# Top-k attention and a gated MLP on one core: a rounding step rewritten, and four steps of a slot reordered

## The chip, the cores and the metric

The kernel runs on one core of a Trainium2 chip. The metric is the device time of one execution in microseconds (us), from the first to the last instruction of the core. The profile is one profiled execution of the same program.

## The reference

Two layers in a row. The first is attention over 8 batches, 8 heads, 576 positions and head size 64, in which each row keeps its 32 largest scores:

```python
scores = scale * np.matmul(q, k.transpose(0, 1, 3, 2))
kth = np.partition(scores, -top_k, axis=-1)[..., -top_k:-top_k + 1]
mask = scores >= kth
scores = np.where(mask, scores, -1000000000.0)
scores = scores - np.max(scores, axis=-1, keepdims=True)
attn = np.exp(scores)
attn = attn / (np.sum(attn, axis=-1, keepdims=True) + 1e-09)
return np.matmul(attn, v).astype(np.float32)
```

The result is laid out as 4608 tokens of 512 values and goes through the second layer, whose weights are 512 x 2048 and 2048 x 512 and come in float64:

```python
h = x @ w_in
g = h * (1.0 / (1.0 + np.exp(-1.702 * h)))
return (g @ w_out).astype(np.float32)
```

## The kernel before

Engines are named PE (TensorE), DVE (VectorE), ACT (ScalarE), POOL (GpSimd) and SP (SyncE, which issues all loads and stores here). Each works through its own queue in program order, and the order of the program is written out by hand: nothing is moved by a scheduler.

**Slots.** The work is cut into 144 slots, 18 for each batch. A slot is 128 query rows of a pair of heads; the last 64 rows of two pairs share an "ends" slot. Even batches run their 16 full slots first and the two ends slots last, odd batches the other way round. The function `slot(n)` issues for each engine what belongs to slot n, in a software pipeline. DVE selects the 32 largest of the rows of slot n (`topk`, 14 operations: MAX8 on L241, MATCH_REPLACE8 on L244, two heads in turn). For slot n-1, POOL makes the two bounds (L260, L261), ACT the exponentials (L269, L271), DVE the division's reciprocal (L280, L282, after topk's operation 5). In the first ten slots POOL then scales an identity (`by`, L286) that the turning on PE multiplies with (L302); from slot SETTLED (9) on ACT and POOL scale the exponentials themselves (L288, L289) and PE turns them (L300). ACT copies the turned blocks out (L310), PE multiplies with the values (L332), ACT copies the result (L344). For slot n+2, PE makes the scores (L225) and ACT copies them out (L232).

**The second layer in the same slots.** When 128 tokens are complete, four slots get a quarter each of the hidden layer (`hidden`, 32 matmuls, L373), at the slot's end. In the next slot ACT takes the tanh (L390) and the gate multiplies it with the hidden values: up to slot 9 and after the last attention slot on DVE straight from PSUM (L406), in between on POOL (L403, L404) after ACT has copied the hidden values (L393). `project` (8 matmuls, L421) comes two slots later at the earliest.

**q and k.** `load` fetches a pair's q or k, `prepare` turns it: four PE transposes into one of the two PSUM buffers of `ps_t` (L193) and one ACT copy (L195). The prepare of k also turns the last 64 positions of q and k together (L199, a second buffer of ps_t) and copies them out (L200, L202). The buffers of ps_t also take the turned blocks and the results of the values, in rotation. A table, READY, says in which slot each is prepared. In even batches every q and k has a slot of its own; in odd batches the third pair's q and k share one slot, and the fourth pair's another:

```python
    READY = (((-9, -8), (-7, -6), (-5, -4), (-3, -2)), ((-7, -6), (-5, -4), (-3, -3), (-2, -2)))
```

From slot 7 on (`settled`), the prepares are issued after topk and ahead of the projection and the turning, and the scores after the values; in slots 0 to 6 the prepares and the scores are issued ahead of topk.

**The weights.** In slots 0 to 8 the float64 weights are rounded to float32, 32 pieces of 128 x 512, three or four a slot (two in slot 0). Their raw words stand in `raws`, 8 buffers; the loads of a slot's pieces are issued one slot ahead. A piece goes through ACT (magnitude of the high word, "size", L142), DVE (shift left by 3, L143, between topk's operations from the eighth on), ACT (L145 "low" and L144 "sign") and, in the next slot, POOL (two operations of 128 x 512, L138 and L139, "finish").

Of the kernel before, what the change touches and what calls it, by code (L numbers as in the profile page):

```python
# [9 lines left out]
ALU = mybir.AluOpType  # L10
ENG = mybir.EngineType
F32 = mybir.dt.float32
U32 = mybir.dt.uint32
# [3 lines left out]
P = 128  # L17
# [11 lines left out]
def kernel(  # L29
# [24 lines left out]
    nc = tc.nc  # L54
# [13 lines left out]
    PIECE = 512  # L68
# [12 lines left out]
    const = ctx.enter_context(tc.tile_pool(name="const", bufs=1))  # L81
# [20 lines left out]

    ident = const.tile([P, P], F32, name="ident")
    make_identity(nc, ident[:])
    win = const.tile([P, CC, DFF], F32, name="win")
    wout = const.tile([P, FC, C], F32, name="wout")

# [14 lines left out]
    def round_piece(n):  # L122

        c, g = pieces[n]
        dst = wout[:, g, :] if c is None else win[:, c, g * PIECE : (g + 1) * PIECE]
        words = raw.pop(n)[:].rearrange("p (n w) -> p n w", w=2)
        low, high = words[:, :, 0], words[:, :, 1].bitcast(F32)
        bits, whole = dst.bitcast(U32), dst.bitcast(I32)

        def finish():
            nc.gpsimd.tensor_tensor(out=whole, in0=whole, in1=low.bitcast(I32), op=ALU.add)  # L138
            nc.gpsimd.tensor_tensor(out=dst, in0=dst, in1=high, op=ALU.mult)  # L139

        return {
            "size": lambda: nc.scalar.activation(dst, high, AF.Abs, scale=REBASE),  # L142
            "shift": lambda: nc.vector.tensor_scalar(bits, bits, 3, None, op0=ALU.logical_shift_left),  # L143
            "sign": lambda: nc.scalar.activation(high, high, AF.Sign),  # L144
            "low": lambda: nc.scalar.mul(out=low.bitcast(I32), in_=low, mul=2.0**-29),  # L145
            "finish": finish,
        }
# [37 lines left out]
    def prepare(name, b, hp):  # L185
        src = loaded.pop((name, b, hp))


        before = 0 if name == "q" else TAIL
        dst = qkt.tile([P, S + before], F32, name=f"{name}_t")  # L190
        full = ps_t.tile([P, 512], F32, name="tp")
        for t in range(NF):
            nc.tensor.transpose(full[:, t * P : (t + 1) * P], src[:, t, :, :], ident[:])  # L193
        scale = SCALE if name == "q" else 1.0
        nc.scalar.mul(out=dst[:, before : before + FULL], in_=full[:], mul=scale)  # L195
        (qT if name == "q" else kT)[b, hp] = dst
        if name == "k":
            ends = ps_t.tile([P, 512], F32, name="tp")
            nc.tensor.transpose(ends[:, 0:P], loaded.pop(("ends", b, hp))[:], ident[:])  # L199
            nc.scalar.mul(out=qT[b, hp][:, FULL:S], in_=ends[:, 0:TAIL], mul=SCALE)  # L200
            for to in (0, before + FULL):
                nc.scalar.copy(out=dst[:, to : to + TAIL], in_=ends[:, TAIL:P])  # L202
# [12 lines left out]
    def scores(n):  # L215
        b, t, hps = slots[n]
        ps = [ps_s.tile([P, 2, 512], F32, name="s_ps") for _ in range(2)]
        if t < NF:
            parts = [(i, 0, slice(0, P), slice(t * P, (t + 1) * P)) for i in range(2)]
        else:  # L220
            parts = [(i, p, slice(p * TAIL, (p + 1) * TAIL), slice(FULL, S)) for i, p in ((0, 0), (1, 1), (0, 1), (1, 0))]
        for c in range(2):
            for i, p, rows, cols in parts:
                on = slice(i * D, (i + 1) * D)
                nc.tensor.matmul(  # L225
                    ps[i][rows, c, 0:HALF],
                    lhsT=qT[b, hps[p]][on, cols],
                    rhs=kT[b, hps[p]][on, FIRST[i] + c * HALF : FIRST[i] + (c + 1) * HALF],
                )
        sc = st[n]["sc"] = scp.tile([P, 2, S], F32, name="sc")  # L230
        for i in range(2):
            nc.scalar.copy(out=sc[:, i, :].rearrange("p (c k) -> p c k", c=2), in_=ps[i][:, :, 0:HALF])  # L232
# [22 lines left out]
    def bounds(n):  # L255

        top = st[n]["top"]
        cut = st[n]["cut"] = small.tile([P, 2], F32, name="cut")
        low = st[n]["low"] = small.tile([P, 2], F32, name="low")
        nc.gpsimd.tensor_scalar(cut[:], top[:, :, TOPK - 1], -1.0, None, op0=ALU.mult)  # L260
        nc.gpsimd.tensor_tensor(out=low[:], in0=top[:, :, TOPK - 1], in1=top[:, :, 0], op=ALU.subtract)  # L261

    def exponentials(n):

        sc, cut, low = st[n]["sc"], st[n]["cut"], st[n]["low"]
        pr = st[n]["pr"] = prp.tile([P, 2 * S], F32, name="pr")
        den = st[n]["den"] = small.tile([P, 2], F32, name="den")
        for i in range(2):
            nc.scalar.activation(sc[:, i, :], sc[:, i, :], AF.Prelu, bias=cut[:, i : i + 1], alpha=HUGE)  # L269
        for i in range(2):  # L270
            nc.scalar.activation(  # L271
                pr[:, i * S : (i + 1) * S], sc[:, i, :], AF.Exp, bias=low[:, i : i + 1],
                accum_out=den[:, i : i + 1],
            )
# [37 lines left out]
    def turn_main(n):  # L312
        for i in range(2):
            turn(n, i * NF, MAIN[i], NF)

    def turn_ends(n):

        turn(n, 2 * NF, FULL, 1)
# [45 lines left out]
    def hidden():  # L364
        if not ready:
            return
        xT, rows = ready[0]
        g = hidden_at["g"]
        ph = ps_h.tile([P, G, P], F32, name="ph")
        for i in range(G):  # L370
            f = g * G + i
            for c in range(CC):
                nc.tensor.matmul(  # L373
                    ph[:, i, :],
                    lhsT=win[:, c, f * P : (f + 1) * P],
                    rhs=xT[:, c, :],
                    start=(c == 0),
                    stop=(c == CC - 1),
                )
        to_gate.append((ph, g, rows))  # L380
        hidden_at["g"] = (g + 1) % NG
        if g == NG - 1:
            ready.pop(0)
# [58 lines left out]
    by_slot = dict(enumerate([2, 3, 4, 4, 4, 4, 3, 4, 4]))  # L442
# [21 lines left out]
    def slot(n):  # L464
        todo = later.pop(n, [])
        for fn, args in todo:
            if fn is not prepare:
                fn(*args)
        preparing = [args for fn, args in todo if fn is prepare]
        settled = n > PROJECTS  # L470
        aside = SETTLED < n < N
        before = 0 <= n - 1 < N
        if before:
            bounds(n - 1)
            exponentials(n - 1)
        if n < 0:
            for m in range(2):
                for args in preparing:
                    if args[2] == m:
                        prepare(*args)  # L480
                scores(m)
        elif not settled:
            for args in preparing:
                prepare(*args)
            scores(n + 2)
        some = [round_piece(x) for x in by_slot.get(n, [])]
        for piece in some:
            piece["size"]()
        shifts = [piece["shift"] for piece in some]
        tanh(aside)  # L490
        for i, op in enumerate(topk(n) if 0 <= n < N else [lambda: None] * 14):
            op()
            if i == 2 and unfinished:
                unfinished.pop(0)()
            if i == 5:
                if before:
                    divide(n - 1)
                while unfinished:
                    unfinished.pop(0)()
            if i == 11 and not aside:  # L500
                gate(aside)
            if i > 6 and shifts:
                shifts.pop(0)()
        if aside:
            gate(aside)
        if settled:
            for args in preparing:
                prepare(*args)
        for piece in some[:2]:
            piece["low"]()  # L510
        going = settled and len(to_project) > (2 if n < N else 0)
        if going:
            project(range(G - 1))
        if before:
            turn_main(n - 1)
        if going:
            project(range(G - 1, G))
        if before:
            turn_ends(n - 1)
        for piece in some[2:]:  # L520
            piece["low"]()
        if before:
            values(n - 1)
        for piece in some:
            piece["sign"]()
            unfinished.append(piece["finish"])
        if settled and n + 2 < N:
            scores(n + 2)
        hidden()

    with tc.manual_schedule():
        for n in range(-1, N + 1):
            slot(n)
        n = N + 1
# [33 lines left out]
```

## Time and profile before

Three runs took 1666.99, 1668.62 and 1668.85 us, median 1668.62. The profiled execution has a span of 1667.9 us. The busy times of its engines:

| engine | busy us | share of the span | instructions |
|---|---|---|---|
| PE (matmul) | 1599.2 | 96% | 11923 |
| DVE | 1468.8 | 88% | 3210 |
| ACT | 1155.7 | 69% | 2450 |
| POOL | 753.0 | 45% | 785 |

The operations that the change touches, from the groups of instructions:

| line, engine, what | count | mean ns |
|---|---|---|
| L142 ACT size | 32 | 671 and 662 |
| L143 DVE shift of w_in's pieces | 16 | 832 |
| L143 DVE shift of w_out's pieces | 16 | 986 |
| L406 DVE gate | 10 | 680 |
| L193 PE transposes of q and k | 256 | 292 |
| L199 PE transposes of the ends | 32 | 311 |

A line of the timeline gives start and length in us, engine, line, operation, what is written and read, its shape and how often, and in brackets the idle time of the engine ahead of it with what ended that. A line of the list of waits gives who waited for whom: us in total, times, and the longest. A row of busy time by stretch gives the stretch, its length, each engine's busy time in it with the number of instructions, the granted share of PE's clock, the share of the DMA engines and GB/s.

### The profile page before, as it was taken

Reading aid. Unit: us, or ns where it says so; the run is one execution under the profiler, and the core shown is the slowest. Engines: PE = TensorE matmul, PEld = TensorE weight load, DVE = VectorE, ACT = ScalarE, POOL = GpSimd, SP = SyncE. Lnnn points to the kernel's source line nnn. Section 1 sums busy time; section 2 is a strip of 40 time slices with the busy share of each in tenths; the row PEclk is TensorE's granted clock in tenths of the full one; section 3 lists DMA queues with packets and bytes.
Section 4 is the critical chain, followed back from the end, with each engine's and each line's share of the span. In section 5 each row is a group of like instructions: output and inputs, shape, how many; then the busy total and the mean of one; then the engine's idle time right before and its main releaser. Section 6 shows DMA issues by size and latency. Waiting matters only on the chain.

```text
span 1667.9 us, 31998 instructions
## 1 busy us (share of the span) xinstructions
PE 1599.2 (96%) x11923; PEld 1174.2 (70%) x11923; DVE 1468.8 (88%) x3210; ACT 1155.7 (69%) x2450; POOL 753.0 (45%) x785
## 2 busy tenths in 40 slices
PE   5579999999999999999999999999999999999999
PEld 3466767777777767777777776777777776777776
DVE  4999989998999988998899997999899998899980
ACT  5987766677766676667776676667777676777661
POOL 1787434444444443444444443444444444444440
PEclk7789999999999999999999999999999999999999
DMA  7342100110001100111001110011000110000000
GB/s 211 115 151 62 23 23 14 36 36 22 21 8 42 29 22 22 36 28 30 22 7 28 29 36 16 8 36 36 22 21 8 43 29 22 22 7 8 7 8 13
DMA packets 125723, 56.59 MB, mean 34 GB/s; under 512 B 116864, under 2 KB 116864, under 8 KB 125568
## 3 DMA queue, kind: packets, MB, share of 16 engines
q1 hardware_dynamic: 125568, 54.55, 12.4%
q8 instruction: 94, 1.54, 0.4%
q14 instruction: 61, 0.50, 0.1%
HBM read 45.09 MB, written 9.44 MB: 33 GB/s over the span
## 4 chain that ended last, share of the span: by engine, by line
PE 87%; DVE 5%; ACT 5%; SPq 1%; issue 1%; POOL 1%; DMA 0%; POOLq 0%; ACTq 0%
PE ph L373 29%; PE po L421 29%; PE o L332 10%; PE s_ps L225 10%; PE tp L300 8%; DVE top L241 2%; DVE left L244 2%; ACT pr L271 1%; PE tp L193 1%; ACT sc L232 1%; DVE wout L143 1%; ACT sc L269 1%; ACT pr L288 0%; SPq L160 0%; DVE win L143 0%
## 5 line engine op out<-in xcount | busy, mean ns | idle before, releaser
L241 DVE MAX8 top<-left 128x8 f32<-128x576 f32 x864 | 610.0, 746 | 0.0
L289 POOL TENSOR_SCALAR pr<-pr,rden 128x576 f32<-128x576 f32 x135 | 232.9, 1725 | 688.8 <-ACT th L390 640.7
L421 PE MATMUL po<-wout,gT 128*128 128x512 f32 x1152 | 542.4, 594 | 0.0
L373 PEld LDWEIGHTS ph<-xT,win 128*128 128x128 f32 x4096 | 470.6, 193 | 56.0 <-issue 47.6
L373 PE MATMUL ph<-xT,win 128*128 128x128 f32 x4096 | 494.4, 279 | 6.4 <-DVE gT L406 6.4
L244 DVE MATCH_REPLACE8 left<-top,left 128x576 f32<-128x576 f32 x576 | 423.3, 742 | 0.0
L310 ACT COPY pt<-tp 128x512 f32<-128x512 f32 (+1 forms) x432 | 193.4, 481 | 192.0 <-PE tp L300 185.6
L421 PEld LDWEIGHTS po<-wout,gT 128*128 128x128 f32 x1152 | 198.3, 192 | 142.6 <-issue 142.4
L232 ACT COPY sc<-s_ps 128x576 f32<-128x576 f32 x288 | 169.9, 642 | 134.8 <-PE s_ps L225 134.6
L271 ACT ACTIVATE pr<-sc,low 128x576 f32<-128x576 f32 x288 | 219.5, 767 | 0.0
L300 PEld LDWEIGHTS tp<-ident,pr 128*128 128x128 f32 x1215 | 145.0, 140 | 104.7 <-issue 42.3
L269 ACT ACTIVATE sc<-sc,cut 128x576 f32<-128x576 f32 x288 | 208.7, 779 | 9.2 <-POOL cut L260 9.2
L244 DVE MATCH_REPLACE8 left<-top,sc 128x576 f32<-128x576 f32 x288 | 211.6, 742 | 0.0
L241 DVE MAX8 top<-sc 128x8 f32<-128x576 f32 x288 | 201.9, 742 | 10.7 <-ACT sc L232 10.7
L403 POOL TENSOR_SCALAR th<-th 128x512 f32<-128x512 f32 x134 | 200.6, 1497 | 0.0
L225 PE MATMUL s_ps<-k_t,q_t 64*128 64x288 f32 (+1 forms) x1280 | 182.2, 431 | 1.3 <-ACT k_t L195 1.3
L300 PE MATMUL tp<-ident,pr 128*128 128x128 f32 x1215 | 177.2, 273 | 0.3 <-POOL pr L289 0.2
L404 POOL TENSOR_TENSOR gT<-th,h 128x512 f32<-128x512 f32 x134 | 171.5, 1280 | 11.2
L332 PEld LDWEIGHTS o<-pt,v_l 128*64 128x64 f32 x2560 | 128.0, 138 | 67.8 <-ACT pt L310 67.8
L332 PE MATMUL o<-pt,v_l 128*64 128x128 f32 (+1 forms) x2560 | 161.7, 269 | 0.2
L280 DVE TENSOR_SCALAR some<-den 128x2 f32<-128x2 f32 x144 | 24.1, 168 | 130.6 <-ACT pr L271 130.4
L225 PEld LDWEIGHTS s_ps<-k_t,q_t 64*128 64x128 f32 (+1 forms) x1280 | 99.6, 177 | 40.2 <-issue 20.9
(50 smaller groups left out, 1152.3 us busy)
## 6 DMA issues: line engine op xcount, KB each, us to landing
q_l<-in_q_dram SPq DMA_DIRECT2D x64, 128.0 KB, 2.5
k_l<-in_k_dram SPq DMA_DIRECT2D x64, 128.0 KB, 2.6
v_l<-in_v_dram SPq DMA_DIRECT2D x64, 128.0 KB, 2.5
raw<-in_moe_w_in_dram SPq DMA_DIRECT2D x16, 512.0 KB, 4.3
raw<-in_moe_w_out_dram SPq DMA_DIRECT2D x16, 512.0 KB, 3.7
out_dram<-ob SPq DMA_DIRECT2D x32, 256.0 KB, 2.1
ends<-in_q_dram SPq DMA_DIRECT2D x32, 32.0 KB, 2.3
ends<-in_k_dram SPq DMA_DIRECT2D x32, 32.0 KB, 2.4
```

The costliest lines, as they stand in the source:

```text
L225: nc.tensor.matmul(ps[i][rows, c, 0:HALF], lhsT=qT[b, hps[p]][on, cols], rhs=kT[b, hps[p]][on, FIRST[i] + c * HALF : FIRST[i] + (c + 1) * ...
L241: nc.vector.max(top[:, i, 8 * r : 8 * r + 8], (left if r else sc)[:, i, :])
L244: nc.vector.match_replace(left[:, i, :], top[:, i, 8 * r : 8 * r + 8], (left if r else sc)[:, i, :], LOWEST)
L269: nc.scalar.activation(sc[:, i, :], sc[:, i, :], AF.Prelu, bias=cut[:, i : i + 1], alpha=HUGE)
L271: nc.scalar.activation(pr[:, i * S : (i + 1) * S], sc[:, i, :], AF.Exp, bias=low[:, i : i + 1], accum_out=den[:, i : i + 1],)
L289: nc.gpsimd.tensor_scalar(pr[:, S : 2 * S], pr[:, S : 2 * S], rden[:, 1:2], None, op0=ALU.mult)
L300: nc.tensor.transpose(tp[:, c * P : (c + 1) * P], pr[:, at], ident[:])
L310: nc.scalar.copy(out=to, in_=tp[:, 0 : blocks * P])
L332: nc.tensor.matmul(o[j * D : (j + 1) * D, 0 : cols.stop - cols.start], lhsT=main[:, c, j, :] if c < NF else tail[:, j, :], rhs=pt[:, j * N ...
L373: nc.tensor.matmul(ph[:, i, :], lhsT=win[:, c, f * P : (f + 1) * P], rhs=xT[:, c, :], start=(c == 0), stop=(c == CC - 1),)
L403: nc.gpsimd.tensor_scalar(th[:], th[:], 1.0, None, op0=ALU.add)
L421: nc.tensor.matmul(po[:], lhsT=gT[:, i, :], rhs=wout[:, f, :], start=(f == 0), stop=(f == FC - 1))
```

## The change

Four things. The shift of the weights becomes a scalar_tensor_tensor that shifts and then takes the bitwise or with a column of zeros, spread over the piece by a step of zero. In slots 0 to 6 the magnitudes are issued ahead of the prepares of q and k and of the scores, not behind them. The gate on DVE is issued after topk's ninth operation (index 8), not its twelfth (11). From slot 7 on, where a slot prepares two of q and k, the second one is issued after the scores instead of beside the first.

```diff
@@ -102,6 +102,8 @@
     ident = const.tile([P, P], F32, name="ident")
     make_identity(nc, ident[:])
+    none = const.tile([P, 1], U32, name="none")
+    nc.vector.memset(none[:], 0)
     win = const.tile([P, CC, DFF], F32, name="win")
@@ -140,7 +142,10 @@
             "size": lambda: nc.scalar.activation(dst, high, AF.Abs, scale=REBASE),
-            "shift": lambda: nc.vector.tensor_scalar(bits, bits, 3, None, op0=ALU.logical_shift_left),
+            "shift": lambda: nc.vector.scalar_tensor_tensor(
+                out=bits, in0=bits, scalar=3, in1=none[:].to_broadcast([P, PIECE]),
+                op0=ALU.logical_shift_left, op1=ALU.bitwise_or,
+            ),
             "sign": lambda: nc.scalar.activation(high, high, AF.Sign),
@@ -479,13 +484,13 @@
                 scores(m)
-        elif not settled:
+        some = [round_piece(x) for x in by_slot.get(n, [])]
+        for piece in some:
+            piece["size"]()
+        if 0 <= n and not settled:
             for args in preparing:
                 prepare(*args)
             scores(n + 2)
-        some = [round_piece(x) for x in by_slot.get(n, [])]
-        for piece in some:
-            piece["size"]()
         shifts = [piece["shift"] for piece in some]
         tanh(aside)
@@ -497,14 +502,14 @@
-            if i == 11 and not aside:
+            if i == 8 and not aside:
                 gate(aside)
             if i > 6 and shifts:
                 shifts.pop(0)()
         if aside:
             gate(aside)
         if settled:
-            for args in preparing:
+            for args in preparing[:1]:
                 prepare(*args)
         for piece in some[:2]:
             piece["low"]()
@@ -526,6 +531,9 @@
         if settled and n + 2 < N:
             scores(n + 2)
+        if settled:
+            for args in preparing[1:]:
+                prepare(*args)
         hidden()
```

## The prediction

> **What bounds the kernel now.** I read the chain of waits on the page, then busy time by stretch, then the list of waits after 160 us, and last the timelines around the waits that this pointed to.
>
> ```profile
> PE 87%; DVE 5%; ACT 5%; SPq 1%; issue 1%; POOL 1%; DMA 0%; POOLq 0%; ACTq 0%
> ```
>
> TensorE (PE) sets the end for most of the span. Busy time by stretch (PE, PEld, DVE, ACT, POOL, clock, DMA) shows two regimes:
>
> ```profile
> 120.00:130.00 10.00, 7.77 (x72) 6.29 (x71) 10.00 (x19) 8.41 (x17) 6.73 (x8) 1.00 0.62 162
> ...
> 150.00:160.00 10.00, 10.00 (x78) 7.27 (x76) 7.76 (x18) 6.78 (x15) 6.44 (x8) 1.00 0.00 0
> ```
>
> Up to about 150 us, slots 0 to 9, VectorE (DVE) is full and PE has holes; here the weights are rounded. Afterwards PE is full (98 to 100% in stretches of 200 us), so there only holes on PE count. The list of waits after 160 us has one on PE that matters:
>
> ```profile
> PE tp L199 <- ACT q_t L195: 13.6, 8, 1.9
> ```
>
> Eight waits: in each odd batch the third and fourth pairs of heads have q and k prepared in one slot, 4 x 2. The timelines of PE and of ScalarE (ACT) at the first:
>
> ```profile
> 213.62 0.60 PE L193 MATMUL tp<-ident,k_l 128*128 128x128 f32 x4
> 215.88 0.33 PE L199 MATMUL tp<-ident,ends 128*128 128x128 f32 x1 [1.67 <-ACT q_t L195]
> 216.05 2.74 PE L421 MATMUL po<-wout,gT 128*128 128x512 f32 x6
> ```
>
> ```profile
> 214.55 0.79 ACT L288 ACTIVATE pr<-pr,rden 128x576 f32<-128x576 f32 x1
> 215.23 0.60 ACT L195 ACTIVATE q_t<-tp 128x512 f32<-128x512 f32 x1
> ```
>
> q's and k's transposes fill both buffers of ps_t. The transposes of the ends need a buffer back, and its copy stands on ACT behind exponentials, tanh, h and L288. k's four transposes have been issued by 214.06 (four take 0.44, as 213.18 to 213.62 for q), so PE loses 215.88 - 214.06 = 1.82 us, with the projection queued behind. The slot lasts 13.43 us; the slot before, with k alone, 11.11.
>
> In the first slots, DVE at slot 0, then DVE and POOL at slot 3:
>
> ```profile
> 24.85 0.43 DVE L143 TENSOR_SCALAR win<-win 128x512 uint32<-128x512 uint32 x1 [8.55 <-ACT win L142]
> ```
>
> ```profile
> 62.93 1.54 DVE L143 TENSOR_SCALAR win<-win 128x512 uint32<-128x512 uint32 x1
> 64.39 0.75 DVE L241 MAX8 top<-left 128x8 f32<-128x576 f32 x1
> 65.06 0.85 DVE L143 TENSOR_SCALAR win<-win 128x512 uint32<-128x512 uint32 x1
> ```
>
> ```profile
> 62.88 1.30 POOL L138 TENSOR_TENSOR win<-win,raw 128x512 int32<-128x512 int32 x1
> 64.26 1.36 POOL L139 TENSOR_TENSOR win<-win,raw 128x512 f32<-128x512 f32 x1
> 65.59 1.46 POOL L138 TENSOR_TENSOR win<-win,raw 128x512 int32<-128x512 int32 x1
> ```
>
> A shift beside an idle POOL takes 0.43, beside a busy one 0.8 to 1.5. The shift begun at 62.93 ends at 64.47, 0.29 after POOL's operation (64.18); that of 65.06 ends at 65.91, 0.29 after the next (65.62), and POOL's following operation stretches from 1.30 to 1.46. They take turns.
>
> **The skill.** "SBUF — State Buffer", section "Who interferes with whom": DVE and GpSimd share one port pair; tensor_scalar in a two-port mode takes it, and whoever starts second is blocked. The trace agrees (0.43 against 0.85 and 1.54). The same section says that a DVE instruction with two SBUF inputs contends with a GpSimd operation that reads SBUF, and one with at most one does not. The new shift reads bits and none, both in SBUF; L138 and L139 read SBUF. For the one-input half the trace agrees: the gate L406, a scalar_tensor_tensor of the same size whose second input is PSUM, takes 0.67 to 0.69 beside a busy POOL. Of two inputs no row shows anything. "VectorE: DVE Perf Modes", section "Mode 2×_2P": two results a cycle only with no second tensor, so the new shift streams at half rate.
>
> **The change part by part**, summed against the profiled span of 1667.9; the three runs (1666.99 to 1668.85) lie about 0.7 above it.
>
> 1. Second q or k behind the scores. Removes 8 x 1.82 = 14.6 us of PE's wait. All of k's part moves: five transposes (0.6 us of PE, same work), four copies on ACT (0.9 us); no DMA is issued in it. At the new place the two buffers last held the turned ends and the values; their copies end before or during the scores (xT at 222.19, scores issued until 222.94), so the ends don't wait. The cost is on ACT: the next slot's exponentials start 0.9 later, and behind them DVE's division, POOL's L289 and the turning. From the end of the scores, PE needs 0.6 (k) + 3.7 (hidden) + 0.44 (q) + 2.57 (projection) = 7.3 us to the turning and 7.7 to its second half; ACT's L288 ends at 1.24 + 0.9 + 2.86 + 0.94 + 0.79 = 6.7, L289 at 7.3. That is hidden. After the second of the two slots no q follows: 6.85 and 7.29, nothing to spare; I charge 0.1 x 4. The loads that reuse the buffers of k come several slots later, so SP doesn't wait. Sum -14.2, bounds -15 and -7 (the whole 0.9 exposed eight times).
>
> 2. Magnitudes first. Slot 0: the raw pieces land by 15.6 (issued at 10.5 and 11.1, 4.3 to 5.0 to landing), q only at 17.5, so ACT does the two magnitudes in its idle time after 15.2 and DVE's waits of 8.55 and 2.61 go. Most of this isn't kept: slot 2 is held by ACT. The exponentials of slot 0 start at 26.4, not 30.07 (signs end 1.1 earlier); in slot 1 three magnitudes (1.7) now precede the copies of q and k, so the scores start 3.7 - 1.7 = 2.0 earlier, and a PE wait of 0.66 behind those copies mostly goes. DVE's division of slot 1 (47.55 now) comes about 2.2 earlier. Slot 6 loses a wait of 1.62 on a magnitude. In other slots the copies only trade places; the last raw piece of a slot lands 3.8 after POOL's last finishing operation frees its buffer, and its magnitude stands 0.3 + 2.9 + 1.7 = 4.9 after it, so ACT doesn't start to wait for the load. Sum -3.8, bounds -5 and -2.
>
> 3. The shift. The five of slots 0 and 1 lie before ACT's bound. In slots 2 to 8 there are 27, on DVE's full path. Below: no contention, 0.60 each from start to start (L406's pitch) where four take 1.46 + 0.78 + 0.77 + 0.72 now: -1.27 a slot of four, -0.8 in the slot of three, -8.4. ACT then binds (12.7 to 13 us of work a slot against 12.4 of DVE) and about 1.5 comes back: -7. Above: it takes turns as now and streams 512 elements at one a cycle, twice 0.27: +0.27 x 27 = +7.3, POOL's operations pushed back with it. I take the skill's side and +0.22, since it names only reads as contended and POOL's last writes may overlap: +5.9.
>
> 4. Gate after the ninth operation, slots 5 to 9. Same work. PE's waits for it (2.2 in slots 7 and 8) go, but slot 9 is held by POOL's finishing, then L260, exponentials and L288 until 160.5, so that buys nothing: 0. What it adds: DVE, with three shifts and five operations behind, may wait for tanh; if shifts are 0.6, it arrives 3.0 after the exponentials' end and tanh ends at 3.9 in slot 5 (sizes and score copies ahead). With slow shifts it doesn't. Bounds -1 and +3 (it can move a shift to just behind a POOL operation's start).
>
> 5. The memset of one column: DVE is idle until 10.66. 0.
>
> Sum: -14.2 - 3.8 + 5.9 = -12.1, span 1655.8, runs **1656.5**.
>
> **Rivals.**
> - The broadcast column doesn't contend: -14.2 - 3.8 - 7 = -25, **1644**. For it: L406's 0.67. Against it: the skill, and both inputs lie in SBUF. Chance 0.25.
> - It contends at the present price: -18, **1650.5**. Chance 0.15.
> - A new wait takes the place of the old: exponentials 0.9 later are exposed at the turning in all eight slots, 7.2 back: **1663.5**. Against it: the slack of 0.4 above. Chance 0.08.
> - Slower: shifts lose the race. The gate and longer shifts move the shifts in phase; one that arrives just after POOL's next operation has begun waits it out, 1.3 us. Ten of 27 misses eat 12.1, twelve make it slower, fourteen give -12.1 + 18.2 = +6, **1675**. Against it: now only each slot's first shift waits so long, and DVE has 0.67 of work between two shifts where POOL's operation takes 1.3. Chance 0.04.
> - That the shift edit doesn't take it off the port is my forecast itself.
>
> **How the numbers follow.** Forecast 0.48, own range 1652 to 1661 (shift +0.1 to +0.35, gate's phase). The range 1642 to 1663 takes in the cheap shift and stops short of the exposed wait's end and the slow case. A measurement of this kernel tells about 0.2%, 3.3 us, from no change. All but the slow case and a combination of lost gains lie below 1665: faster 0.93, same 0.03, slower 0.04.
>
> **What would show it.** Step 1: no wait of L199 on q_t after 160 us, slots of 11.6 instead of 13.43. Step 2: DVE's first shift near 16.3, the division of slot 1 near 45.3. Step 3: shifts of 0.9 to 1.7 us beside POOL, POOL's operations up to 1.75; if they are 0.6 to 0.7 throughout, the first rival is right. The start of slot 9's top-k, now near 142.0, would be at 144 with my price, at 131 to 132 without contention. PE waits in turning (L300) behind L289 or L288 would prove the third rival; a gain under 8 us would prove me wrong on step 1.

## The result, and the profile after

The changed kernel takes 1658.72 us (median of 4 runs, 1658.09 to 1659.03), the kernel before 1668.45 (4 runs). The ratio is 0.9943, 95% interval 0.9926 to 0.996: 9.7 us faster, where 12.1 were forecast. Below, each kernel's ratio is to the kernel before, timed beside it on the same chip. A run's time is 1.8 us longer than the span of the same execution in the profile (1658.09 beside 1656.3, and 1669.71 beside 1667.9 for the profiled execution of before).

The chain of waits of the changed kernel, for comparison with the first line shown of before:

```profile
PE 90%; DVE 7%; ACT 1%; SPq 1%; issue 0%; DMA 0%; POOL 0%; POOLq 0%; ACTq 0%
```

PE's share went up from 87% to 90% and DVE's from 5% to 7%; ACT's fell from 5% to 1%. The first slots have become longer on DVE, as busy time by stretch (columns as before) shows:

```profile
120.00:130.00 10.00, 9.62 (x72) 7.71 (x73) 10.00 (x15) 8.00 (x17) 6.66 (x6) 0.83 0.48 151
...
150.00:160.00 10.00, 8.08 (x59) 6.67 (x60) 9.97 (x24) 3.07 (x8) 8.50 (x8) 0.83 0.00 0
```

From 150 to 160 us DVE is still full and PE has holes, where PE was full before. Slot 9's top-k starts 4.65 us later. To find where the difference arose I laid the starts of every slot's top-k (the first MAX8 that reads sc) of both traces side by side, each counted from its own slot 0. Slot 0 itself began at 11.03 instead of 10.66; this varies from execution to execution (10.96 in the first experiment below, which leaves the first slots as they were).

| start of slot | before | whole change | difference |
|---|---|---|---|
| 1 | 18.98 | 10.86 | -8.11 |
| 2 | 32.59 | 27.59 | -5.01 |
| 5 | 73.75 | 73.18 | -0.57 |
| 7 | 102.84 | 104.09 | +1.24 |
| 9 | 131.35 | 135.62 | +4.27 |
| 16 | 208.91 | 213.20 | +4.28 |
| 18 | 235.77 | 236.52 | +0.74 |
| 19 to 52 | | | +0.69 |
| 143 | 1599.93 | 1587.87 | -12.05 |

DVE's first shift now starts at 16.59 instead of 24.85, without a wait, which gives the 8 us in the first slot. The next eight slots eat this gain and turn it into a loss of 4.3. Part of that is a wait for ACT's exponentials in slot 1:

```profile
16.59 0.68 DVE L145 SCALAR_TENSOR_TENSOR win<-win,none 128x512 uint32<-128x512 uint32 x1
...
29.49 0.17 DVE L285 TENSOR_SCALAR some<-den 128x2 f32<-128x2 f32 x1 [3.42 <-ACT pr L276]
```

From slot 9 to the end the difference moves only in the slots that prepare both q and k, by -3.6 in three of the four odd batches. In the remaining one (slots 52 to 54) the profiled execution of before lost 2.0 us more, at a granted PE clock of 0.83 from 620 to 630 us. Its wait there was 1.95 us instead of 1.67, and the six matmuls of the projection behind it took 4.42 instead of 2.74:

```profile
623.38 0.39 PE L199 MATMUL tp<-ident,ends 128*128 128x128 f32 x1 [1.95 <-ACT q_t L195]
623.56 4.42 PE L421 MATMUL po<-wout,gT 128*128 128x512 f32 x6
```

With -3.6 everywhere, 4 x -3.6 + 4.65 = -9.7, the difference of the medians; the spans of the two profiled executions differ by 11.6. Nine executions of the kernel before, timed beside the first experiment, fall in two groups, five at 1668.1 to 1668.6 and four at 1670.1 to 1670.2, so a loss of about this size may come in some executions and not in others (only one was profiled).

PE at the first slot of two, after:

```profile
217.83 0.60 PE L198 MATMUL tp<-ident,q_l 128*128 128x128 f32 x4
218.27 2.74 PE L426 MATMUL po<-wout,gT 128*128 128x512 f32 x6
...
225.16 0.66 PE L198 MATMUL tp<-ident,k_l 128*128 128x128 f32 x4
225.65 0.27 PE L204 MATMUL tp<-ident,ends 128*128 128x128 f32 x1
225.76 3.74 PE L378 MATMUL ph<-xT,win 128*128 128x128 f32 x32
```

None of them has a bracket with a wait. k's transposes and the ends' follow the scores back to back, the hidden layer follows the ends after 0.11 us. The next slot's q comes at 229.33, so the slot lasts 11.50 us instead of 13.43 (the start-to-start gain differs a little from slot to slot, 1.8 on average). The list of waits after 160 us has no line of PE on L204 at all. On ACT the exponentials now stand behind the copies of k and the ends, as the forecast had it:

```profile
226.40 0.62 ACT L200 ACTIVATE k_t<-tp 128x512 f32<-128x512 f32 x1
226.89 0.25 ACT L205 ACTIVATE q_t<-tp 128x64 f32<-128x64 f32 x1
226.99 0.36 ACT L207 COPY k_t<-tp 128x64 f32<-128x64 f32 x2
227.18 1.49 ACT L274 ACTIVATE sc<-sc,cut 128x576 f32<-128x576 f32 x2
```

The copies begin at 226.40 and the exponentials at 227.18, at most 0.78 us later than without them, and PE doesn't wait for that: the waits of the turning (L305) on exponentials or on POOL's scaling sum to 0.2 us after 160 us, as before.

The loss, in slot 5. DVE first, then POOL:

```profile
90.00 1.80 DVE L145 SCALAR_TENSOR_TENSOR win<-win,none 128x512 uint32<-128x512 uint32 x1
91.73 0.75 DVE L246 MAX8 top<-left 128x8 f32<-128x576 f32 x1
92.40 0.66 DVE L411 SCALAR_TENSOR_TENSOR gT<-th,ph 128x512 f32<-128x512 f32 x1
92.98 1.77 DVE L145 SCALAR_TENSOR_TENSOR win<-win,none 128x512 uint32<-128x512 uint32 x1
94.68 0.75 DVE L246 MAX8 top<-left 128x8 f32<-128x576 f32 x1
95.35 1.11 DVE L145 SCALAR_TENSOR_TENSOR win<-win,none 128x512 uint32<-128x512 uint32 x1
```

```profile
89.96 1.29 POOL L140 TENSOR_TENSOR wout<-wout,raw 128x512 int32<-128x512 int32 x1
91.33 1.63 POOL L141 TENSOR_TENSOR wout<-wout,raw 128x512 f32<-128x512 f32 x1
92.92 1.28 POOL L140 TENSOR_TENSOR wout<-wout,raw 128x512 int32<-128x512 int32 x1
94.29 1.63 POOL L141 TENSOR_TENSOR wout<-wout,raw 128x512 f32<-128x512 f32 x1
```

The first shift begins at 90.00, 0.04 after POOL's operation, and ends at 91.80, 0.55 after that operation's end (91.25); with the old shift it was 0.29. POOL's next is stretched to 1.63. The gate, which has the same opcode and size and reads PSUM, takes its usual 0.66 beside POOL. But it moves the second shift to 92.98, 0.06 behind the start of POOL's next operation, and the shift waits all of it out: 1.77 instead of 1.11.

### The profile page after: what moved, and what is told of

It is laid out like the page before. It is cut to its first block, busy times and chain, and to the rows that moved or that the text cites. A ratio compares the mean times of both kernels' runs of the same rounds, so it can differ in the third digit from the quotient of the medians.

```text
span 1656.3 us, 32011 instructions
## 1 busy us (share of the span) xinstructions
PE 1597.5 (96%) x11923; PEld 1174.0 (71%) x11923; DVE 1481.2 (89%) x3211; ACT 1154.2 (70%) x2450; POOL 758.4 (46%) x785
## 4 chain that ended last, share of the span: by engine, by line
PE 90%; DVE 7%; ACT 1%; SPq 1%; issue 0%; DMA 0%; POOL 0%; POOLq 0%; ACTq 0%
PE ph L378 31%; PE po L426 29%; PE o L337 10%; PE s_ps L230 10%; PE tp L305 8%; DVE top L246 3%; DVE left L249 2%; PE tp L198 2%; DVE wout L145 1%; DVE win L145 1%; PE tp L307 0%; SPq L165 0%; DMA k_l<-in_k_dram 0%; ACT pr L276 0%; PE tp L204 0%
## 5 line engine op out<-in xcount | busy, mean ns | idle before, releaser
L305 PEld LDWEIGHTS tp<-ident,pr 128*128 128x128 f32 x1215 | 144.8, 141 | 105.9 <-issue 41.5
L274 ACT ACTIVATE sc<-sc,cut 128x576 f32<-128x576 f32 x288 | 209.0, 781 | 13.9 <-POOL cut L265 13.9
L305 PE MATMUL tp<-ident,pr 128*128 128x128 f32 x1215 | 178.1, 273 | 0.3 <-POOL pr L294 0.2
```

Of the source, the lines that this page charges most:

```text
L305: nc.tensor.transpose(tp[:, c * P : (c + 1) * P], pr[:, at], ident[:])
```

## The experiments

All of these but the first have the text of the changed kernel as their base. The lengths of shifts are those of the profile; the starts of slots are counted from each kernel's own slot 0, as in the table above.

**The reordering of q and k alone.** The kernel before with only this:

```diff
-            for args in preparing:
+            for args in preparing[:1]:
                 prepare(*args)
...
             scores(n + 2)
+        if settled:
+            for args in preparing[1:]:
+                prepare(*args)
         hidden()
```

> The kernel before with the second q or k behind the scores alone. Mine: the eight waits of PE go, 8 x 1.8 us, and the first slots stay as before: 1668.5 - 14.3 = 1654.2 us (1653.2 to 1655.2), faster than the whole change. Rival, that the first slots' edits bring nothing or a little and the reordering gives only the 10 us measured: 1658.7 or more.

Measured: 1653.36 us beside 1668.59, ratio 0.9903 (0.9888 to 0.9918), 15.2 us faster. Slot by slot, the first slots are those of before (within 0.1 us up to slot 16), then slots 16 and 17 gain 1.6 and 1.9. The reordering alone beats the whole change by 5 us; the other three parts together cost time.

**The old shift in the whole change.**

```diff
-            "shift": lambda: nc.vector.scalar_tensor_tensor(
-                out=bits, in0=bits, scalar=3, in1=none[:].to_broadcast([P, PIECE]),
-                op0=ALU.logical_shift_left, op1=ALU.bitwise_or,
-            ),
+            "shift": lambda: nc.vector.tensor_scalar(bits, bits, 3, None, op0=ALU.logical_shift_left),
```

> The whole change with the old shift (tensor_scalar). Mine: the new shift costs about 0.26 us more each from start to start over 27 shifts, so 6 to 7 us come back: 1652 us (1649 to 1654); shifts beside POOL again 0.8 to 1.5 us. The shift behind the gate still waits out one POOL operation. Rival, that the loss in the first slots comes from the order of magnitudes and gate and not from the shift: 1657.5 to 1659.

Measured: 1651.28 us, ratio 0.9894 (0.988 to 0.9907), 17.3 us faster than before and so 7.6 better than with the new shift. Slot 9 starts 2.5 us earlier than before, not 4.3 later. The shift behind the gate still waits out a POOL operation (1.51 instead of 0.85).

**The zeros in PSUM.** Same opcode, same first input, but the second input comes from PSUM for the pieces of slots 0 to 6:

```diff
+    zeros = ps_p.tile([P, C], F32, name="zeros", tag="po")
+    nc.vector.memset(zeros[:].bitcast(U32), 0)
+    LATE = 24
...
-                out=bits, in0=bits, scalar=3, in1=none[:].to_broadcast([P, PIECE]),
+                out=bits, in0=bits, scalar=3, in1=zeros[:].bitcast(U32) if n < LATE else none[:].to_broadcast([P, PIECE]),
...
-                proj["po"] = ps_p.tile([P, C], F32, name="po")
+                proj["po"] = ps_p.tile([P, C], F32, name="po", tag="po")
```

> The whole change, but the zeros lie in PSUM for the pieces of slots 0 to 6 (in the bank that the projection takes from slot 7), in SBUF for slots 7 and 8. Mine: with one SBUF input the same operation no longer takes turns with POOL: 0.60 to 0.70 us each in slots 2 to 6, still 1.0 to 1.8 in slots 7 and 8; start of slot 7's top-k 10 us earlier than with the whole change, of which ACT and POOL give some back: 1649 us (1646 to 1652). Rival, that the operation itself is slow beside a busy POOL: shifts stay at 1.0 us and more, 1658.7.

Measured: 1649.51 us, ratio 0.9882 (0.9869 to 0.9896). DVE in slot 6, the last with PSUM, and slot 7, the first with SBUF:

```profile
101.48 0.68 DVE L149 SCALAR_TENSOR_TENSOR wout<-wout,zeros 128x512 uint32<-128x512 uint32 x1
102.75 0.67 DVE L149 SCALAR_TENSOR_TENSOR wout<-wout,zeros 128x512 uint32<-128x512 uint32 x1
112.25 1.80 DVE L149 SCALAR_TENSOR_TENSOR wout<-wout,none 128x512 uint32<-128x512 uint32 x1
```

One operation in one kernel, and between the rows one difference: the second input is a full tile of zeros in PSUM, or the repeated column in SBUF. The repetition itself costs nothing where POOL is idle (0.67 and 0.68 in slot 0 of the changed kernel). All shifts of slots 0 to 6 take 0.67 or 0.68, 22 of them beside an operation of POOL, as in the rows above. Slot 7 starts 8.65 us earlier than with the whole change (95.44 against 104.09), and slot 4 lasts 12.9 us, the length that the forecast gave a slot without contention. It is not ACT alone that holds it there: DVE waits 0.46 us for ACT's exponentials, and ACT 0.3 to 0.6 for POOL's bounds, which need DVE's result: a ring of the three engines.

**POOL writes and reads nothing.** Here POOL's two operations on a piece are replaced, which leaves the rounding of the weights unfinished:

```diff
-            nc.gpsimd.tensor_tensor(out=whole, in0=whole, in1=low.bitcast(I32), op=ALU.add)
-            nc.gpsimd.tensor_tensor(out=dst, in0=dst, in1=high, op=ALU.mult)
+            for _ in range(4):
+                nc.gpsimd.memset(dst, 0.0)
```

> The whole change, but POOL's two finishing operations on a piece are replaced by four memsets of it, which read nothing; the rounding of the weights is left unfinished. Mine, from the skill's words that two inputs contend only with a POOL operation that reads: shifts of 0.60 to 0.70 us throughout beside a POOL busy with memsets. Rival, that the shift locks against any POOL operation: shifts of 0.8 us and more where a memset runs.

Measured in one execution, of 1640.95 us: all 32 shifts take 0.67 to 0.69, 28 of them beside a memset. DVE and POOL in slot 2:

```profile
46.56 0.68 DVE L145 SCALAR_TENSOR_TENSOR win<-win,none 128x512 uint32<-128x512 uint32 x1
...
47.83 0.67 DVE L145 SCALAR_TENSOR_TENSOR win<-win,none 128x512 uint32<-128x512 uint32 x1
```

```profile
46.50 4.49 POOL L141 MEMSET win<- 128x512 f32 x8
```

POOL is busy without a gap from 46.50 to 50.99 and the shifts with both inputs in SBUF run through. A memset of a piece takes about 0.56 us where a finishing operation takes 1.29, so POOL writes more here than in the changed kernel. What is gone is its reading, and the contention goes with it.

**The gate back behind the twelfth operation.**

```diff
-            if i == 8 and not aside:
+            if i == 11 and not aside:
```

> The whole change with the gate back behind topk's twelfth operation. Mine: in slots 5 to 8 the shift behind the gate no longer arrives just after a POOL operation began, 0.67 us each: 1656 us (1655 to 1657.5). Rival, that the early gate helps since PE's hidden layer starts earlier: 1660 to 1661.

Measured: 1656.63 us, ratio 0.9924 (0.9911 to 0.9936), 12.0 faster than before and 2.2 better than the whole change. DVE in slot 5:

```profile
90.09 1.80 DVE L145 SCALAR_TENSOR_TENSOR win<-win,none 128x512 uint32<-128x512 uint32 x1
91.81 0.75 DVE L246 MAX8 top<-left 128x8 f32<-128x576 f32 x1
92.48 1.11 DVE L145 SCALAR_TENSOR_TENSOR win<-win,none 128x512 uint32<-128x512 uint32 x1
```

The second shift takes 1.11 again, in each of slots 5 to 8, where it took 1.75 to 1.79. So moving the gate forward cost time. The intervals of the two ratios overlap, but every run of this kernel (1655.91 to 1656.77) is below every run of the whole change (1658.09 to 1659.03), and slot 9 starts 2.1 us earlier in the trace.

**The magnitudes back behind the copies.**

```diff
-        some = [round_piece(x) for x in by_slot.get(n, [])]
-        for piece in some:
-            piece["size"]()
         if 0 <= n and not settled:
             for args in preparing:
                 prepare(*args)
             scores(n + 2)
+        some = [round_piece(x) for x in by_slot.get(n, [])]
+        for piece in some:
+            piece["size"]()
```

> The whole change with the magnitudes back behind the copies of q and k and the scores. Mine: the waits of slots 0, 1 and 6 come back, 3.4 us at slot 1's division and 1.6 in slot 6: 1663 us (1661.5 to 1664.5). Rival, that the magnitudes' place buys nothing since ACT, and not DVE, holds the first slots: 1658.7.

Measured: 1662.93 us, ratio 0.9964 (0.9952 to 0.9977), only 6.0 faster than before, so the magnitudes' place is worth 3.7 us when each kernel is set against the kernel before timed with it. The medians themselves differ by 4.2, the starts of slot 9 in the traces by 5.1. DVE's list of waits up to 160 us has the old line again:

```profile
DVE win L145 <- ACT win L144: 11.3, 2, 8.7
```

That is slots 0 and 1. The wait of slot 6 on a magnitude did not come back, though I had expected it: with the early gate it is absent from this kernel too, and with the late gate and early magnitudes it is absent as well.

**Gate ahead of the shifts, old shift.** On top of the old shift, tanh is issued ahead of the magnitudes and the gate behind topk's seventh operation, ahead of the slot's first shift (the edit of the shift is the one above):

```diff
+        tanh(aside)
         some = [round_piece(x) for x in by_slot.get(n, [])]
...
         shifts = [piece["shift"] for piece in some]
-        tanh(aside)
...
-            if i == 8 and not aside:
+            if i == 6 and not aside:
```

> The whole change with the old shift, tanh ahead of the magnitudes and the gate behind topk's seventh operation, ahead of the slot's first shift. Mine: the first shift of a slot waits for POOL anyway, so the gate's 0.6 us lies in that wait, and the second shift is no longer pushed behind another POOL operation: slots 5, 7 and 8 last 13.6 us instead of 14.5 to 14.9, 1646.6 us (1645 to 1648.5). Rival, that the place of the gate costs nothing and only the number of shifts does: 1651, as with the old shift alone.

Measured: 1647.84 us, ratio 0.9874 (0.9859 to 0.9889). That is 3.4 us below the old shift alone. Slots 5, 7 and 8 last 13.6 to 13.9 us. DVE in slot 5:

```profile
86.44 0.68 DVE L408 SCALAR_TENSOR_TENSOR gT<-th,ph 128x512 f32<-128x512 f32 x1
...
87.76 0.94 DVE L145 TENSOR_SCALAR win<-win 128x512 uint32<-128x512 uint32 x1
...
89.30 0.85 DVE L145 TENSOR_SCALAR win<-win 128x512 uint32<-128x512 uint32 x1
```

The first shift after the gate takes 0.94 instead of 1.53, the second 0.85 instead of 1.51: the gate lies in a wait that was there anyway. Tanh moved together with the gate; the two were not separated.

**Zeros in PSUM and the gate ahead of the shifts.** Both together, with the old shift in slots 7 and 8, where the bank belongs to the projection (only the new part of the edit is shown):

```diff
+        def shift():
+            if n < LATE:
+                nc.vector.scalar_tensor_tensor(
+                    out=bits, in0=bits, scalar=3, in1=zeros[:].bitcast(U32),
+                    op0=ALU.logical_shift_left, op1=ALU.bitwise_or,
+                )
+            else:
+                nc.vector.tensor_scalar(bits, bits, 3, None, op0=ALU.logical_shift_left)
...
+            "shift": shift,
```

> The zeros in PSUM for slots 0 to 6, the old shift in slots 7 and 8, tanh first and the gate behind the seventh operation. Mine: 1645 us (1643.5 to 1647): slots 2 to 6 at ACT's 12.9 us, slots 7 and 8 at 13.6. Rival, that ACT or POOL holds every slot already: 1649 as with the zeros in PSUM alone.

Measured: 1643.71 us, ratio 0.985 (0.9837 to 0.9864): the fastest of all, 25 us below the kernel before and 15 below the changed one. Slot 9 starts 9.8 us earlier than before.

## Why the prediction was right

The medians are 1656.5 forecast and 1658.7 measured. The spans agree more closely, 1655.8 and 1656.3, but that is luck: the profiled execution of before, from which the sum was taken, held the extra loss of 2.0 us. The 0.7 us that the forecast added from span to run mixed different executions; in the same one it is 1.8. The fair comparison is a gain of 12.1 against 9.7. By the forecast's own steps, with the trace column taken from the starts of slot 9 after each kernel's own slot 0 (for step 1 from the slots that prepare both, without the loss of 2.0):

| step | forecast | by medians | in the traces | by what |
|---|---|---|---|---|
| 1, second q or k last | -14.2 | -15.2 | -14.4 | alone |
| 2, magnitudes first | -3.8 | -3.7 | -5.05 | undone |
| 3, the new shift | +5.9 | +7.6 | +6.74 | undone |
| 4, the gate at the ninth | 0 | +2.2 | +2.09 | undone |
| sum | -12.1 | -9.1 | -10.6 | whole: -9.7 and -10.1 |

Steps 2 to 4 were measured with the others in place, so the sums need not meet the whole exactly.

**Step 1** was right in mechanism and size. The wait was read from one timeline (1.82 us) and its eightfold from one line of the list of waits; the copies moved on ACT had slack behind them, and none of the later exponentials reaches PE.

**Step 2** came out close to its sum, partly by luck. Its first term was larger: slot 1's division comes at 44.17, 3.4 us earlier and not 2.2. The exponentials ahead of it start at 41.19 instead of 44.56, behind a turning on PE that begins 1.9 us earlier, which is close to the 2.0 forecast, and lasts 2.55 instead of 3.55. That last us was not in the forecast. It fits the granted clock, whose mean over the turning is 0.79 instead of 0.55 (2.55 x 0.79 and 3.55 x 0.55 are both 2.0). The second term can't be laid to step 2 alone: undoing step 2 did not bring slot 6's wait back. It also goes with the early gate.

**Step 3** was right in the side it took and a little low. The Trainium skill's sentence on two SBUF inputs ("SBUF — State Buffer", "Who interferes with whom") held in both halves: with one input in PSUM there was no contention (0.67 us), and none beside a POOL that only writes (0.67 to 0.69). The discount from +0.27 to +0.22, for POOL's last writes, was wrong: the shift ends 0.55 after POOL's operation, which is the 0.29 of before plus the full 0.26 of the slower stream. 27 x 0.27 would have been 7.3.

**Step 4** is where the sum missed most. "So that buys nothing: 0" was half right. PE's waits for the gate went and were replaced by waits for `by`, the identity that POOL scales behind DVE's division, so there was no gain: from 90 to 160 us PE waited 6.4 us in four waits for the gate before, and 12.2 in four for `by` after. With the gate back behind the twelfth operation it is the gate again, 8.3 in four. In slot 9:

```profile
151.92 3.65 PE L307 MATMUL tp<-by,pr 128*128 128x128 f32 x16 [4.08 <-POOL by L291]
```

But the bound named beside it, a shift moved to just behind a POOL operation's start, is what happened, in each of slots 5 to 8: 1.70 us from start to start instead of 1.03. Four times 0.67 is 2.7; undoing it gave 2.2. The old timeline would have allowed to work this out: after the first shift DVE had 0.67 us of work and POOL some 1.1 left of its operation; with the gate DVE has 1.27.

Steps 3 and 4 together also show in the sign that the forecast named: slot 9's top-k starts at 146.65, not at 144.

Of the rivals, no contention (1644) is refuted, and with it contention at the old price; the exposed exponentials did not occur. The slower rival's mechanism, a shift that loses the race, did occur: four times, not the twelve that it needed. The first rival's sum has a slip: four shifts at 0.60 against 3.73 save 1.33 a slot, not 1.27, so -8.8 and not -8.4 before ACT binds. The third rival's 7.2 on top of 1656.5 is 1663.7.

What stays open: the kernel before lost 2 us in one profiled execution at a lower granted clock, beside one of the eight stalls. Whether stalls on PE bring that about was not tried. If some executions have this loss and others do not, it would explain why the reordering gains 15.2 by the medians and 14.4 slot by slot; that is not shown.

## What to carry to other kernels

A change of four parts is priced part by part, and a net gain says nothing of each part: here one part gave 15 us, one about 4, and two cost 10 together. When two engines take turns, as DVE's shifts and POOL's operations do here, the price of an operation is not only its length but where it arrives in the other's cycle. The gate between two shifts made the second one wait out an operation of POOL; put ahead of the shift that waits anyway, it cost next to nothing. An edit that is to end contention has to be priced on both sides: the old shift, with one input, contended (0.8 to 1.5 us), the new one with both inputs in SBUF contended longer, and the same new one with its second input in PSUM did not.

## What the runs showed of the hardware

- A scalar_tensor_tensor of 128 x 512 with both inputs in SBUF, one of them a single column repeated by a step of zero, takes 0.67 us beside an idle POOL and 1.05 to 1.81 beside a POOL that reads SBUF. The repeated column is enough of a second input for that.
- It ends 0.55 us after the operation of POOL that it met; the old tensor_scalar ends 0.29 after.
- It delays POOL too: POOL's following operation takes 1.62 to 1.76 instead of 1.29.
- With the second input in PSUM, or beside memsets on POOL, the same operation takes 0.67 to 0.69.
